# Weight loads of the later experts no longer wait for the rows' transposes, and the planner counts loads, maxima and gathers as ready later

## The chip, the cores and the metric

The kernel runs on one core of a Trainium2 chip. The metric is the device time of one execution in microseconds (us), as the median of several runs. The engines are named as in the profile: PE (TensorE, matmuls), DVE (VectorE), ACT (ScalarE), POOL (GpSimd) and SP (SyncE, which here issues DMAs).

## The reference

A linear attention with a norm, whose output is the input of a mixture of experts; each token goes to one of eight experts with limited places.

```python
kv = np.einsum('bhsd,bhse->bhde', k, v)
out = np.einsum('bhsd,bhde->bhse', q, kv)
rms = np.sqrt(np.mean(out * out, axis=-1, keepdims=True) + 1e-06)
x = out / rms * g_norm                      # N = 4608 tokens of D = 512
...
logits = x @ w_gate
expert_idx = np.argmax(logits, axis=1)      # E = 8
...
h = np.maximum(np.einsum('ecd,edf->ecf', disp, w1), 0.0)   # F = 1024
y = np.einsum('ecf,efd->ecd', h, w2)
...
out[i] = gate_w[i] * y[expert_idx[i], pos[i]]
```

`disp` holds the tokens of each expert, at most capacity of them; the softmax of the logits gives `gate_w`.

## The kernel before

The first third of the span is attention, norm and the routing of tokens. Then the experts follow, ranked by their number of tokens, r = 0 to 7, with a budget of 704 down to 544 rows. Each product is made in two halves of 16 bits: a value is split into a high and a low part, and of the four products three are made (high by high, low by high, high by low).

For expert r, `products(r)` makes the first products `Gemm1`: eight columns of 128 hidden values, each of 24 matmuls over half of the rows (16 with `w1h`, then 8 with `w1l`) into a buffer `hp`. ACT makes `hh` of it (the high part after the maximum with 0), DVE `hl` (the low part). There are two buffers `hp`, so a third column begins only when `hl` of the first is done. Then the second products follow, in tiles of 24 matmuls of 512 columns into one of two banks `yp`; ACT scales a tile into `ysb`, and POOL scatters it to `out` by the places `si`. The last, narrower tile is made turned: `products` of small matmuls, a copy `yt` by DVE and a transpose by PE.

Beside it runs what the next expert needs. `weights(r + 1)` loads `raw1` and `raw2` in four parts each on SP's queue (512 KB a load, L312), takes the maximum of each part on DVE (`am` L328, then `a` L336 and L338 over the parts), turns it across the partitions on PE (`across`, `pt_max` L341), takes the maximum of that on DVE (`bm` L345, `across_max`) and spreads it on PE (`back`, `pt_max` L348); from it DVE makes the scale (`bmax`, `ew`, `p2t`, `sw`, `sg`). With the scale ACT makes the high parts `w1h`, `w2h` (L362) and DVE the low parts `w1l`, `w2l` (L368). There is one buffer for each part of `raw1` and `raw2`.

`rows_beside(r + 1)` gathers the rows of the next expert in blocks of 128: POOL gathers `xg` by a DMA, POOL makes the norm `xm`, ACT casts `pair` (high, L456), POOL makes its low part (L460), and SP transposes `pair` by a DMA into `xs` (L464). `xm` has one buffer, `pair` two, `xg` three. DVE copies the gate `gt` (L437).

What stands in which order on each engine is fixed before the program runs by a planner, `Plan.place`: it is given operations with a cost, dependencies and a key, takes for each engine the one that can begin first (by the key among those that are ready), and counts its end as its start plus its cost, and its readiness for another engine as that end plus a lag. Its outcome is only an order for each engine; on the chip each engine works its own row off, waiting by semaphores. Operations with the key FIRST are taken as soon as they count as ready.

Of the kernel before, what the change touches and what calls it, by code (L numbers as in the profile page):

```python
# [36 lines left out]
LAG = {("T", "T"): 0.0, ("A", "T"): 0.27, ("A", "V"): 0.15, ("V", "P"): 0.16, ("V", "A"): 0.15, ("A", "A"): 0.14,  # L37
       ("V", "V"): 0.13, ("P", "P"): 0.1, ("D", "D"): 0.0, ("D", "T"): 1.1, ("D", "V"): 1.1, ("D", "P"): 1.1, ("D", "A"): 1.1,
       ("P", "D"): 0.3, ("S", "D"): -0.6, ("T", "S"): 0.2}
LAG_ELSE = 0.21  # L40
# [19 lines left out]
WKEYS = ((29.5, 0.3), (38.0, 0.3))  # L60
ON_X = 0


class Hold:

# [14 lines left out]
class Op:  # L80
    def __init__(self, ways, fn, deps, takes, key):
        self.ways, self.fn, self.deps, self.takes, self.key = ways, fn, deps, takes, key
        self.todo, self.next, self.end = 0, [], None


class Plan:
# [14 lines left out]
    def place(self):  # L101
        for n, o in enumerate(self.ops):
            o.n = n
            deps = set(o.deps)
            for h in o.takes:
                if h.before:
                    deps.update(h.before.users)
            o.deps = deps
            for d in deps:
                d.next.append(o)  # L110
            o.todo = sum(d.end is None for d in deps)
        free, order = dict(self.free), []
        ready = {e: [] for e in free}

        def enter(o):
            o.at = {e: max([d.end + LAG.get((d.eng, e), LAG_ELSE) for d in o.deps], default=0.0) for e, _ in o.ways}
            for e, t in o.ways:
                ready[e].append((o, t))

        for o in self.ops:  # L120
            if not o.todo:
                enter(o)
        while len(order) < len(self.ops):
            best = None
            for e, cands in ready.items():
                mine = []
                for o, t in cands:
                    at = max(free[e], o.at[e])
                    if all(at + t <= max(free[f], o.at[f]) + u for f, u in o.ways):
                        mine.append((at, o.at[e] if e in FIFO else o.key, o.n, o, t))  # L130
                if mine:
                    at = min(mine)[0]
                    if best is None or at < best[0]:
                        best = (at, e) + min(x[1:] for x in mine if x[0] <= at + WAIT.get(e, 0.0))
            at, e, _, _, o, t = best
            o.start = max(free[e], o.at[e])
            o.end = free[e] = o.start + t
            o.eng = e
            for f, _ in o.ways:
                ready[f] = [x for x in ready[f] if x[0] is not o]  # L140
            order.append(o)
            for x in o.next:
                x.todo -= 1
                if not x.todo:
                    enter(x)
        self.free = free
        return sorted(order, key=lambda o: (o.start, o.n))
# [8 lines left out]
def attention_moe_kernel(  # L156
# [1318 lines left out]
    def weights(r, key, after):  # L1475

        ws, sets, zs, holds = wsets[r % 2], [], [], []
        for i in range(2):
# [9 lines left out]
            for p in range(4):  # L1488
                o = op(("S", 0.7), lambda e, i=i, p=p, regs=regs: load(e, i, p, regs),
                       [regs.get("op"), early["rank"]] + after + (early["free"][p] if r == 1 and i == 0 else []), key,  # L1490
                       (raws[p],))
                regs.setdefault("op", o)
                loads.append(op(("D", 1.46), None, [o], key, (), (raws[p],)))
            key += 1
            tops = []
            for p in range(8):
# [10 lines left out]
                f["across"](x.t[:, 128:256])  # L1507

            o = op(("V", 0.3), lambda e, f=f: f["most"](), tops, FIRST)
            o = op(("T", 0.12), across, [o], FIRST, (x,))  # L1510
            o = op(("V", 0.2), lambda e, f=f, x=x: f["across_max"](x.t[:, 128:256]), [o], FIRST, (), (x,))
            o = op(("T", 0.03), lambda e, f=f, x=x: f["back"](x.t[:, 0:1]), [o], FIRST, (), (x,))
            ew = new(f"e{i}")
            o = op(("V", 1.1), lambda e, f=f, x=x: f["scale"](x.t[:, 0:1]), [o], FIRST, (ew,), (x,))
# [10 lines left out]
    def rows_beside(r, key):  # L1525
# [9 lines left out]
        for i in range(n):  # L1535
# [7 lines left out]
            o = op(("P", 1.05), fetch, [cut_, first], key, (hold, xg), (sl,))  # L1543
            first = first or o
            o = op(("D", 0.85), None, [o], key, (), (xg,))
            a = op(("P", 1.0), lambda e, i=i: st["x"].norm(i, nc.gpsimd), [o], key + 1, (xm,), (xg,))
            gates.append(op(("V", 0.07), lambda e, i=i: st["x"].gate(i), [o], key + 1, (), (xg, hold)))
            a = op(("A", 0.52), lambda e, i=i: st["x"].pair_high(i), [a], key + 1, (pair,), (xm, hold))
# [58 lines left out]
    for r in range(E):  # L1607
        products(r, *args)
        key = KEY * r
        if r + 1 < E:  # L1610
            sets, zs, w_holds = weights(r + 1, key + 1, sent)
            st, xs_hold, sl, gates, turned, sent = rows_beside(r + 1, key + ROWS)
            args = (lambda st=st: st["x"], turned, turned, gates, xs_hold, lambda st=st: st["si"], sl, sets, zs, w_holds, 0,
                    BUDGET[r + 1])
        else:
            steps, o = plan_rest(), None
            for _ in range(60):
                o = op(("V", 0.2), lambda e: next(steps, None), [o], key + 1)
# [36 lines left out]
```

## Time and profile before

| | |
|---|---|
| median of 3 runs | 613.12 us (611.6 to 616.77) |
| profiled execution | 612.04 us |
| its span in the trace | 610.2 us |
| mean granted clock of TensorE | 0.976 |
| PE busy | 539.9 us (88%) |
| DVE busy | 388.0 us (64%) |
| ACT busy | 258.5 us (42%) |
| POOL busy | 225.1 us (37%) |

Busy times are of the profiled execution, with shares of its span. The median of three runs stands 1.08 us over the profiled one. The shares are averages over stages with different limits, so the single stages are read from the rows below, in which all times count from the span's start.

### The profile page before, as it was taken

Reading aid. Unit: us, or ns where it says so; the run is one execution under the profiler, and the core shown is the slowest. Engines: PE = TensorE matmul, PEld = TensorE weight load, DVE = VectorE, ACT = ScalarE, POOL = GpSimd, SP = SyncE. Lnnn points to the kernel's source line nnn. Section 1 sums busy time; section 2 is a strip of 40 time slices with the busy share of each in tenths; the row PEclk is TensorE's granted clock in tenths of the full one; section 3 lists DMA queues with packets and bytes.
Section 4 is the critical chain, followed back from the end, with each engine's and each line's share of the span. In section 5 each row is a group of like instructions: output and inputs, shape, how many; then the busy total and the mean of one; then the engine's idle time right before and its main releaser. Section 6 shows DMA issues by size and latency. Waiting matters only on the chain.

```text
span 610.2 us, 12003 instructions
## 1 busy us (share of the span) xinstructions
PE 539.9 (88%) x4535; PEld 368.0 (60%) x4535; DVE 388.0 (64%) x1026; ACT 258.5 (42%) x500; POOL 225.1 (37%) x273
## 2 busy tenths in 40 slices
PE   1988989778978987998999899989999999999990
PEld 1887978666535554645764465567477558658650
DVE  2495787999959998889897298059638905102100
ACT  0564767487413922716443515241552534112110
POOL 6002243255336882456308321812652370010010
PEclk9998999999999988999999989999999999999996
DMA  8999999845169687795804750573357141010010
GB/s 217 297 304 334 331 329 367 266 139 212 69 185 333 125 254 173 194 281 128 309 2 117 219 193 15 137 255 119 78 162 277 37 115 22 0 68 5 0 55 8
DMA packets 94654, 102.71 MB, mean 168 GB/s; under 512 B 51650, under 2 KB 76226, under 8 KB 93568
## 3 DMA queue, kind: packets, MB, share of 16 engines
q1 hardware_dynamic: 86528, 70.50, 41.6%
q0 software_dynamic: 8064, 31.40, 14.9%
q8 instruction: 37, 0.61, 0.4%
q14 instruction: 25, 0.20, 0.1%
HBM read 73.20 MB, written 20.68 MB: 154 GB/s over the span
## 4 chain that ended last, share of the span: by engine, by line
DVE 24%; PE 17%; issue 16%; DMA 12%; POOL 7%; ACT 2%; SPq 1%; POOLq 0%; DVEq 0%; ACTq 0%
PE hp L513 9%; DMA out_dram<-ysb,si 6%; DVE am L328 5%; PE yp L559 5%; DVE w2l L368 5%; DVE w1l L368 4%; DVE hl L521 3%; DMA xs<-pair 3%; POOL pair L460 2%; DMA raw<-in_moe_w_dram 2%; DMA xg<-x_dram,gi 2%; POOL out_dram L589 1%; POOL xm L432 1%; PE yp L568 1%; PE op L513 1%
## 5 line engine op out<-in xcount | busy, mean ns | idle before, releaser
L513 PE MATMUL hp<-xs,w1h 128*128 128x320 f16 (+6 forms) x960 | 139.5, 298 | 11.3 <-DVE p2t L293 5.8
L513 PEld LDWEIGHTS <-w1h 128*128 128x128 f16 x1024 | 100.7, 99 | 50.0 <-issue 15.3
L559 PEld LDWEIGHTS <-hh 128*128 128x128 f16 x560 | 54.0, 98 | 64.2 <-issue 1.9
L518 ACT ACTIVATE hh<-hp 128x320 f16<-128x320 f32 (+7 forms) x64 | 40.9, 641 | 117.2 <-PE hp L513 102.7
L589 POOL DMA_INDIRECT out_dram<-ysb,si x42 | 43.8, 1042 | 120.8 <-ACT ysb L584 94.3
L328 DVE TENSOR_REDUCE am<-raw 128x1 f32<-128x512 f32 x120 | 76.0, 674 | 18.5 <-DMA raw<-in_moe_w_dram 18.5
L424 POOL DMA_INDIRECT xg<-x_dram,gi x42 | 44.0, 1047 | 111.1 <-DVE gt L437 70.2
L513 PE MATMUL hp<-xs,w1l 128*128 128x320 f16 (+6 forms) x480 | 72.2, 292 | 0.0
L521 DVE SCALAR_TENSOR_TENSOR hl<-hp,hh 128x320 f16<-128x320 f32 (+7 forms) x64 | 47.4, 741 | 35.8 <-ACT hh L518 35.7
L780 PE MATMUL op<-kv_bd,qt 128*128 128x144 f32 (+1 forms) x384 | 57.8, 293 | 9.2 <-ACT o_sb L663 3.9
L559 PE MATMUL yp<-w2h,hh 128*128 128x512 f16 x272 | 65.2, 379 | 0.8 <-ACT ysb L584 0.8
L559 PE MATMUL yp<-w2h,hl 128*128 128x512 f16 x272 | 64.4, 379 | 0.0
L559 PE MATMUL yp<-w2l,hh 128*128 128x512 f16 x272 | 64.3, 379 | 0.0
L513 PEld LDWEIGHTS <-w1l 128*128 128x128 f16 x512 | 50.3, 98 | 16.9
L368 DVE SCALAR_TENSOR_TENSOR w1l<-raw,sg,w1h 128x512 f16<-128x512 f32 x64 | 58.3, 951 | 0.0
L780 PEld LDWEIGHTS op<-kv_bd,qt 128*128 128x128 f32 x384 | 50.0, 194 | 12.9 <-ACT o_sb L663 5.2
L584 ACT ACTIVATE ysb<-yp,ysc 128x512 f32<-128x512 f32 (+5 forms) x41 | 28.0, 683 | 62.3 <-PE yp L559 48.4
L456 ACT CAST pair<-xm 128x512 f16<-128x512 f32 (+5 forms) x36 | 22.2, 616 | 69.0 <-POOL xm L432 55.1
L460 POOL TENSOR_TENSOR pair<-xm,pair 128x512 f16<-128x512 f32 (+5 forms) x36 | 42.9, 1190 | 20.4 <-ACT pair L456 19.8
L574 DVE COPY yt<-yp 128x256 f32<-128x256 f32 (+4 forms) x7 | 2.9, 415 | 73.6 <-PE yp L568 61.3
L432 POOL TENSOR_TENSOR xm<-xg 128x512 f32<-128x512 f32 (+5 forms) x39 | 45.0, 1156 | 11.8 <-DMA xg<-x_dram,gi 10.0
L559 PEld LDWEIGHTS <-hl 128*128 128x128 f16 x280 | 27.2, 98 | 32.7 <-issue 0.9
(242 smaller groups left out, 730.6 us busy)
## 6 DMA issues: line engine op xcount, KB each, us to landing
raw<-in_moe_w_dram SPq DMA_DIRECT2D x64, 512.0 KB
x_dram<-o_sb POOLq DMA_DIRECT2D x8, 1152.0 KB, 4.7
k_sb<-in_k_dram SPq DMA_DIRECT2D x16, 512.0 KB
v_sb<-in_v_dram SPq DMA_DIRECT2D x16, 512.0 KB
q_sb<-in_q_dram SPq DMA_DIRECT2D x16, 512.0 KB
x_dram<-o_sb POOLq DMA_DIRECT2D x8, 144.0 KB, 8.5
k_sb<-in_k_dram SPq DMA_DIRECT2D x16, 64.0 KB
v_sb<-in_v_dram SPq DMA_DIRECT2D x16, 64.0 KB
```

What stands on the lines that cost most here:

```text
L328: nc.vector.tensor_reduce(out=am()[:, p:p + 1], in_=raw[:, sl(p)], axis=AX.X, op=ALU.max, apply_absolute_value=True)
L368: nc.vector.scalar_tensor_tensor(out=wl[:, sl(p)], in0=raw[:, sl(p)], scalar=z["s"], in1=wh[:, sl(p)], op0=ALU.mult, op1=ALU.subtract)
L424: nc.gpsimd.indirect_dma_start(out=self.xg[i][0:n], out_offset=None, in_=x_dram[0:self.rows, :], in_offset=bass.IndirectOffsetOnAxis(ap=se ...
L432: eng.tensor_tensor(out=self.xm[i][0:n].rearrange("p (h d) -> p h d", h=H), in0=xg[:, :, 0:D], in1=xg[:, :, D:D + 1].broadcast_to([n, H, D ...
L460: nc.gpsimd.tensor_tensor(out=pair[0:n, 1], in0=self.xm[i][0:n], in1=pair[0:n, 0], op=ALU.subtract)
L513: nc.tensor.matmul(self.view(hp)[:, u], lhsT=w[:, c, j * P:(j + 1) * P], rhs=x[:, c, u * hw:(u + 1) * hw], start=(t == 0 and c == 0), stop ...
L518: nc.scalar.activation(self.out(self.hh, j), self.view(hp), AF.Relu)
L521: nc.vector.scalar_tensor_tensor(out=self.out(self.hl, j), in0=self.view(hp), scalar=0.0, in1=self.out(self.hh, j), op0=ALU.max, op1=ALU.s ...
L559: nc.tensor.matmul(yp[0:n, 0:DM], lhsT=h[:, j, o:o + n], rhs=w[:, j, :], start=(m == 0), stop=(m == len(self.terms) - 1))
L584: nc.scalar.activation(self.ysb[0:n], yp[0:n, 0:DM], AF.Copy, scale=self.ysc[0:n, i:i + 1])
L589: nc.gpsimd.indirect_dma_start(out=out[:, :], out_offset=bass.IndirectOffsetOnAxis(ap=self.sidx[0:n, col:col + 1], axis=0), in_=ysb[0:n], ...
L780: nc.tensor.matmul(ph.t[:, j * m:(j + 1) * m], lhsT=qt.t[:, i * P:(i + 1) * P], rhs=x, start=True, stop=True)
```

## The change

A constant `LATE` is added, and each operation gets a value `late`, 0 if nothing else is said. The planner adds it to the end of an operation when it works out when the ones that depend on it are ready. It is 4.0 us for the landing of a weight load, 2.0 us for `most` (which makes `a`) and 1.0 us for `across_max` (which makes `bm`), all for the weights of the experts 2 to 7, and 1.1 us for the landing of a gather of rows. And `weights` of the experts 3 to 7 no longer gets `sent`, the transposes of the rows of expert r, as something that its loads wait for.

```diff
+LATE = (4.0, 2.0, 1.0)
...
-        self.todo, self.next, self.end = 0, [], None
+        self.todo, self.next, self.end, self.late = 0, [], None, 0.0
...
-            o.at = {e: max([d.end + LAG.get((d.eng, e), LAG_ELSE) for d in o.deps], default=0.0) for e, _ in o.ways}
+            o.at = {e: max([d.end + d.late + LAG.get((d.eng, e), LAG_ELSE) for d in o.deps], default=0.0) for e, _ in o.ways}
...
                 loads.append(op(("D", 1.46), None, [o], key, (), (raws[p],)))
+                loads[-1].late = LATE[0] if r > 1 else 0.0
...
             o = op(("V", 0.3), lambda e, f=f: f["most"](), tops, FIRST)
+            o.late = LATE[1] if r > 1 else 0.0
             o = op(("T", 0.12), across, [o], FIRST, (x,))
             o = op(("V", 0.2), lambda e, f=f, x=x: f["across_max"](x.t[:, 128:256]), [o], FIRST, (), (x,))
+            o.late = LATE[2] if r > 1 else 0.0
...
             o = op(("D", 0.85), None, [o], key, (), (xg,))
+            o.late = 1.1
...
-            sets, zs, w_holds = weights(r + 1, key + 1, sent)
+            sets, zs, w_holds = weights(r + 1, key + 1, [] if r > 1 else sent)
```

No operation is added or taken away. The lines of the changed kernel stand two to six further down (L312 becomes L314, L521 becomes L523). The orders differ from `products(0)` on, at about 189 us of the span.

The first place is on SP, beside the second products of expert 2: `xs` are the rows of expert 4, `raw1` the first weights of expert 5, `raw2` the last load of expert 4's weights. Before:

```order
L312 DMA raw2_2643<-in_moe_w2_dram 128x2x512
L464 DMA_TRANSPOSE xs_4428<-pair_4485 128x8x128
L1420 TENSOR_LOAD n_i_4517
L1420 ISA x2
L464 DMA_TRANSPOSE xs_4428<-pair_4531 128x8x128
L464 DMA_TRANSPOSE xs_4428<-pair_4579 128x8x128
L464 DMA_TRANSPOSE xs_4428<-pair_4607 128x8x128
L464 DMA_TRANSPOSE xs_4428<-pair_4629 128x8x80
L1485 TENSOR_LOAD perm_i_145
L1485 ISA x2
L312 ISA
L312 DMA raw1_149<-in_moe_w1_dram 128x1024
```

In the changed kernel the same stretch of SP:

```order
L314 DMA raw2_2643<-in_moe_w2_dram 128x2x512
L1487 TENSOR_LOAD perm_i_145
L1487 ISA x2
L314 ISA
L314 DMA raw1_149<-in_moe_w1_dram 128x1024
...
L314 DMA raw1_149<-in_moe_w1_dram 128x1024
L466 DMA_TRANSPOSE xs_4422<-pair_4495 128x8x128
L314 ISA
L314 DMA raw1_149<-in_moe_w1_dram 128x1024
L1422 TENSOR_LOAD n_i_4434
```

Three of the four loads of `raw1` now stand ahead of the first transpose, the fourth behind it; the other four transposes follow.

The second place is on DVE at the start of the products of expert 3, where `am0`, `a1_0` and `bm` belong to the weights of expert 5, `w2l` to those of expert 4, and `hl` to the first column. Before:

```order
L437 COPY gt_4429<-xg_4529 80x1
L328 TENSOR_REDUCE am0_4676<-raw1_149 128x1 x2
L368 SCALAR_TENSOR_TENSOR w2l_0_153<-raw2_2643,sw1_4439,w2h_0_152 128x512 x5
L521 SCALAR_TENSOR_TENSOR hl_4738<-hp_4678,hh_4737 128x624
L293 TENSOR_SCALAR p2t_4763<-ew0_3831 128x1
```

In the changed kernel the same place on DVE:

```order
L439 COPY gt_4423<-xg_4549 80x1
L330 TENSOR_REDUCE am0_4553<-raw1_149 128x1 x2
L338 TENSOR_REDUCE a1_0_4640<-am0_4553 128x1
L340 TENSOR_TENSOR a1_0_4640<-a1_0_4640,gcol_124 128x1
L347 TENSOR_REDUCE bm_4670<-pt_max_4664 1x1
L370 SCALAR_TENSOR_TENSOR w2l_0_153<-raw2_2643,sw1_4504,w2h_0_152 128x512 x5
L523 SCALAR_TENSOR_TENSOR hl_4752<-hp_4693,hh_4751 128x624
```

The other six `am0` of the eight stand further ahead of this piece; before, they came between the `hl` of this expert's later columns.

The third place is on DVE in the first products of expert 1, where `am0`, `a1_0`, `am1` and `bm` belong to the weights of expert 2; the first `hl` of the piece before is that of the third column (`hp_3406`). Before:

```order
L328 TENSOR_REDUCE am0_3319<-raw1_149 128x1 x3
L1344 TENSOR_REDUCE nt_3453<-big_3367 128x9
L336 TENSOR_REDUCE a1_0_3455<-am0_3319 128x1
L338 TENSOR_TENSOR a1_0_3455<-a1_0_3455,gcol_124 128x1
L521 SCALAR_TENSOR_TENSOR hl_3351<-hp_3406,hh_3350 128x672
L328 TENSOR_REDUCE am1_3337<-raw2_2643 128x1 x2
L345 TENSOR_REDUCE bm_3482<-pt_max_3471 1x1
```

In the changed kernel, where `hp_3409` is the third column and `hp_3444` the fourth:

```order
L523 SCALAR_TENSOR_TENSOR hl_3363<-hp_3409,hh_3362 128x672
L330 TENSOR_REDUCE am0_3407<-raw1_149 128x1 x3
L1351 TENSOR_TENSOR upto_3344<-upto_3344,nt_3345 128x1
L338 TENSOR_REDUCE a1_0_3491<-am0_3407 128x1
L340 TENSOR_TENSOR a1_0_3491<-a1_0_3491,gcol_124 128x1
L523 SCALAR_TENSOR_TENSOR hl_3363<-hp_3444,hh_3362 128x672
L330 TENSOR_REDUCE am1_3420<-raw2_2643 128x1 x2
L1351 TENSOR_TENSOR upto_3344<-upto_3344,nt_3345 128x1
L439 COPY gt_3050<-xg_3367 128x1
L1351 TENSOR_TENSOR upto_3344<-upto_3344,nt_3345 128x1 x2
L347 TENSOR_REDUCE bm_3532<-pt_max_3518 1x1
```

`a1_0` and `bm` each stand one column later on DVE. On PE `across` moves from within the fourth column to behind the fifth, `back` from between the fourth and the fifth into the sixth; and the transposes of `yt` of expert 0, which stood behind the first column of expert 1, now stand ahead of it.

## Rows read from the trace of the kernel before

**Rows 1.** Windows: span, length, each engine's busy time, PEclk (granted clock), DMA share, GB/s.

```profile
216.60:255.00 38.40, 32.75 (x209) 21.02 (x206) 32.71 (x77) 18.05 (x29) 21.24 (x18) 0.91 0.78 194
...
287.70:341.77 54.07, 53.85 (x329) 31.43 (x325) 41.81 (x93) 21.46 (x34) 21.82 (x20) 1.00 0.46 145
341.77:399.16 57.39, 53.77 (x392) 34.14 (x391) 31.50 (x70) 22.10 (x35) 21.81 (x20) 0.97 0.49 142
```

**Rows 2.** Timeline of PE, first products of expert 1: start, us, operation, [idle before, releaser].

```profile
218.94 3.98 PE L513 MATMUL hp<-xs,w1h 128*128 128x336 f16 x15 [2.03 <-DMA xs<-pair]
...
238.79 0.38 PE L348 MATMUL pt_max<-bm,ones 1*128 1x1 f32 x2 [3.04 <-DVE bm L345]
239.10 4.09 PE L513 MATMUL hp<-xs,w1h 128*128 128x336 f16 x16
...
244.21 2.44 PE L513 MATMUL hp<-xs,w1h 128*128 128x336 f16 x16
```

**Rows 3.** Windows behind three of PE's idle times.

```profile
238.79:242.98 4.19, 4.18 (x18) 2.46 (x19) 4.02 (x13) 2.47 (x4) 1.21 (x2) 0.61 0.44 97
...
351.90:355.60 3.70, 3.68 (x16) 2.15 (x16) 3.56 (x11) 0.00 (x0) 0.00 (x0) 0.56 0.69 226
218.94:222.75 3.81, 3.81 (x16) 2.12 (x17) 3.74 (x13) 0.00 (x0) 2.56 (x3) 0.55 0.77 237
```

**Rows 4.** Timeline of PE, second products of expert 1.

```profile
269.92 0.38 PE L348 MATMUL pt_max<-bm,ones 1*128 1x1 f32 x2 [0.83 <-DVE bm L345]
...
271.96 1.89 PE L559 MATMUL yp<-w2h,hh 128*128 128x512 f16 x8
...
276.15 0.27 PE L341 MATMUL pt_max<-ident,a 128*1 128x128 f32 x1 [0.57 <-DVE a L336]
...
278.40 0.38 PE L348 MATMUL pt_max<-bm,ones 1*128 1x1 f32 x2 [1.11 <-DVE bm L345]
```

**Rows 5.** Timeline of PE, first products of the experts 3, 4 and 5.

```profile
344.95 2.28 PE L513 MATMUL hp<-xs,w1h 128*128 128x312 f16 x16
...
351.92 3.91 PE L513 MATMUL hp<-xs,w1h 128*128 128x312 f16 x16 [3.62 <-DVE p2t L293]
...
407.49 2.17 PE L513 MATMUL hp<-xs,w1h 128*128 128x296 f16 x16 [1.69 <-DVE p2t L293]
...
411.28 2.17 PE L513 MATMUL hp<-xs,w1h 128*128 128x296 f16 x16 [0.61 <-DVE hl L521]
...
465.11 2.12 PE L513 MATMUL hp<-xs,w1h 128*128 128x288 f16 x16 [0.97 <-DVE hl L521]
```

**Rows 6.** Timeline of DVE, first products of the experts 3, 4 and 5.

```profile
346.56 1.28 DVE L328 TENSOR_REDUCE am<-raw 128x1 f32<-128x512 f32 x2 [14.38 <-DMA raw<-in_moe_w_dram]
347.75 3.39 DVE L368 SCALAR_TENSOR_TENSOR w2l<-raw,sw,w2h 128x512 f16<-128x512 f32 x5
...
403.41 0.69 DVE L328 TENSOR_REDUCE am<-raw 128x1 f32<-128x512 f32 x1 [3.38 <-DMA raw<-in_moe_w_dram]
...
463.04 0.35 DVE L623 COPY si<-sidx_tab 128x6 int32 x1 [2.20 <-DMA out_dram<-ysb,si]
```

**Rows 7.** Timeline of SP's DMA issues: start, time from the first issue to the last.

```profile
324.06 16.84 SPq L464 DMA_TRANSPOSE xs<-pair  x5
342.07 14.11 SPq L312 DMA_DIRECT2D raw<-in_moe_w_dram  x8
```

**Rows 8.** Timeline of ACT, first products of the experts 1 and 3.

```profile
235.24 0.62 ACT L456 CAST pair<-xm 128x512 f16<-128x512 f32 x1 [6.56 <-DMA xs<-pair]
...
342.56 3.17 ACT L362 ACTIVATE w2h<-raw,sw 128x512 f16<-128x512 f32 x5
```

**Rows 9.** The chain that ended last: start, us, what.

```profile
222.82 12.32 DMA xs<-pair
...
236.51 0.86 DVE hl L521
...
494.30 3.12 DMA xs<-pair
```

## Prediction

> **What bounds the kernel now.** I read the windows first, by expert. From 216.60 us on, when the experts ranked 1 to 7 follow each other, TensorE (PE) works almost without a break: 53.85 of 54.07 us beside expert 2, 53.77 of 57.39 beside expert 3, but only 32.75 of 38.40 in the first products of expert 1 [rows 1]. In the fullest of these windows VectorE (DVE) has 41.81 of 54.07, so PE sets the pace, and the only time to win after 216 us is where PE stands still or runs at the lower of its two clocks. I therefore went through PE's timeline for the idle times in brackets, and from each to the engine named as its releaser.
>
> Three places stand out. In the products of expert 1, PE waits 2.03 us for the first rows, then 3.04 us for the maximum `bm` [rows 2]. In the second products of expert 1 it waits 0.83, 0.57 and 1.11 us for `bm` and `a` [rows 4]. Then each of the experts 3, 4 and 5 has a wait in its first columns: 3.62, 1.69 and 0.61, 0.97 us [rows 5]. After two of these idle times the clock falls as well: the 16 matmuls that take 2.44 us at 244.21 took 4.09 behind the wait of 3.04, with a granted clock of 0.61; those that take 2.28 at 344.95 took 3.91 behind the wait of 3.62, with 0.56 (of the level of 2.4 GHz, so near that of 1.2) [rows 2, 3, 5]. Behind the wait of 1.69 us 16 matmuls of 296 columns took 2.17, as usual [rows 5].
>
> Where the long waits come from is read on DVE. At 346.56 its queue had been standing for 14.38 us at a maximum `am` whose weight load had not landed; behind it came five `w2l` (3.39 us), and only then `hl`, which frees the first buffer `hp`, which PE wants for its third column [rows 6]. SP shows why the load was late: its eight loads were issued from 342.07 on, behind the five transposes that began at 324.06 [rows 7]. At 403.41 the same `am` wait is 3.38 us [rows 6].
>
> **Experts 3 and 4: the waits for a load.** With the dependency gone three of the four `raw1` loads stand ahead of the first transpose on SP, and with the new late times the planner puts all eight `am`, `a1` and `bm` ahead of the `w2l`. The data is loaded some 15 to 20 us sooner (in the place of transposes from 324.06 on, instead of 342.07 [rows 7]), so the `am` has its data while the second products of the expert before still run, and DVE was idle for those 14.38 us. What is late next: `w2l` needs `w2h` from ScalarE (ACT), whose five run from 342.56 for 3.17 us [rows 8], so the fifth `w2l` ends near 345.7 + 0.7 = 346.4 (3.39 us for five is 0.7 each) and `hl` 0.8 later at 347.2. PE's second column ends at 351.92 - 3.62 = 348.3, so 1.1 us are left, and the whole wait goes. Expert 3: 3.62 + (3.91 - 2.28) for the clock = 5.25, 5.3 with the eight `w1l` behind it that ran a little slow too. Expert 4: 1.69 + 0.61 = 2.3. Nothing in these two sums is on another engine's path.
>
> **Expert 5.** Here DVE stood 2.20 us for a scatter to `out` that still read the old `si`, then did two `am`, and `hl` came late by 0.97 us [rows 6, 5]. The wait for the scatter is not touched; the two `am` (1.27 us) move ahead to the second products before. I take the whole 0.97 as 1.0. Bounds: 0, if the scatter alone makes `hl` late, and 1.0.
>
> **Second products of expert 1.** The waits add to 0.83 + 0.57 + 1.11 = 2.51 us [rows 4]. The late times move `across` and `back` some 12 to 16 matmuls (2.6 to 3.5 us) further back on PE, which covers each of them, if DVE does not come later too. DVE is the tight engine here, its `am` waiting for loads that still follow rows' transposes (expert 3's are issued earlier, but their buffer is freed by `w1l` of expert 2). I take 1.5, bounds 0 and 2.5.
>
> **First products of expert 1.** PE's wait of 3.04 us is for `bm`, which sits on DVE behind `hl` of the third column (236.51 to 237.37) and two `am` [rows 2, 9]. In the new order `across` comes after the fifth column and `back` within the sixth, so the fifth column no longer stands behind `bm` but only behind the third `hl`, at 237.4 instead of 239.10: 1.7 us. That `hl` stays where it was: ACT stood 6.56 us at a cast for a transpose that was issued at 222.82 behind five loads and took 12.32 us, with the `hh` of this column queued behind the cast [rows 8, 9]; nothing in this part of SP's order changes. The fourth column ended at 239.10 - 0.31 - 3.04 = 235.75, so PE now waits 1.6 us there, and since 1.69 us left the clock alone [rows 5] and 2.03 us did not (0.55 after it [rows 3]), I count the slow 16 matmuls as saved: 4.09 - 2.44 = 1.65. Together 3.4. Bounds: 0, if the wait stays over 2 us and the clock falls, or the maxima now wait inside the next columns; 5, if the whole wait with its clock goes. One step here is against the change: the transposes of `yt` of expert 0 now stand ahead of the first column, and `yt` is copied on DVE behind `w2l`, so PE may start its first column later than 218.94. Up to 1.6 us of that cost nothing, since they only shorten the wait for the third `hl` at 237.4; what is more comes off the 3.4, one for one, within its bounds.
>
> **Expert 2.** Its window has 0.22 us of idle PE to give [rows 1], and receives eight `am` of 0.64 us (half of the 1.28 for two [rows 6]) from the window behind: DVE goes from 41.81 to about 46.9 of 54.07. I count a loss of 0.4, bounds 0 and 1.5 (two `hl` late by one `am` each). The 1.1 us by which gathers count as late move only where their readers stand in the queues; POOL and its DMAs keep their order, and I price it at 0.
>
> **The sum.** 5.3 + 2.3 + 1.0 + 1.5 + 3.4 - 0.4 = 13.1 us. The profiled execution took 612.04 us (span 610.2 and 1.84 around it), 1.08 under the median of 613.12. So 612.04 - 13.1 = 598.9, and 613.12 - 13.1 = 600.0 as a median. With every bound at its best it is 5.3 + 2.3 + 1.0 + 2.5 + 5 = 16.1, so 597.0; with the open ones at their worst 5.3 + 2.3 + 0 + 0 + 0 - 1.5 = 6.1, so 607.
>
> **Rivals.** *The transposes are late instead.* Three sets of transposes (rows of experts 4, 5, 6) now queue behind three or four loads of 512 KB. One behind five loads took 12.32 us, one alone 3.12 [rows 9]. `pair` has two buffers, so the third cast on ACT waits for the first transpose; transposes are 16.84 / 4 = 4.2 us apart [rows 7], so the cast is due 8.4 us after the first one's issue and would wait 3.9. Behind it ACT holds an output `ysb`, and PE with its two buffers `yp` can run one tile of 24 matmuls further, under 3 x 1.89 = 5.7 us [rows 4]. So 3.9 us alone are hidden. It decides if SP, at a load whose buffer the last `w1l` have not yet freed, stands for more than 6 us besides: more than a whole set of eight such DVE operations (0.7 each). At 8 us PE would wait 3.9 + 8 - 5.7 = 6.2, with a slow clock (1.65) 7.9 for each of three experts: 23.6 - 13.1 gives 10.5 slower, 623.6. Against it: the window of expert 3 has DMA engines busy for 0.49 only [rows 1], and the `w1l` are done well before the transposes begin. The Trainium skill has a rule on this side: by "DMA: Bandwidth & Descriptors", section "Queues, rings and completion order", what SP issues lies on one ring on each of the DMA engines and is taken in ring order, so a transpose cannot pass the loads ahead of it. The 12.32 us row agrees with it; by it each of the three sets would be delayed as that row was, which is the 3.9 us above.
>
> *Only the experts 3 to 5 gain.* In expert 1 the order of maxima and `hl` is so dense that what leaves one place waits in the next: the third `hl` and the gather of expert 2's rows are unmoved. Then 5.3 + 2.3 + 1.0 = 8.6 and 604.5.
>
> *The change doesn't do what it says.* The `am` comes early, but `hl` is late all the same, since the `w2l` ahead of it are paced by `w2h`: from the margin of 1.1 us above, it takes only a `w2h` group that begins 1.2 us later than 342.56 for the wait to return. Then experts 3 and 4 keep theirs, and with 1.5 or less from the rest the time is 611 to 613.
>
> **How the numbers follow.** The forecast of 600.0 gets 0.63, the gain in experts 3 to 5 alone (604.5) 0.20, no effect (612) 0.12, late transposes (623.6) 0.05. 1% of this kernel is 6.1 us, about what a measurement of it can tell from no change; so faster by over 1% means under 607.0: nearly all of the first case and most of the second, with some of the spread off, 0.77; within 1% what is left of these and the third, 0.18; slower 0.05. The range leaves the last two cases out, and reaches from 595.5 (the best sum, 597.0, less the 1.5 by which the fastest run of before lies under the median) to 608.5 (the worst sum, 607.0, and the same).
>
> **What would show it.** In the trace of the changed kernel: no wait of PE in the third column of experts 3 and 4, and a clock of 1.00 there; `am` on DVE without a long wait for `raw` between 332 and 347; the loads of experts 5, 6 and 7 ahead of the transposes on SP, and these longer, with ACT's casts waiting for `xs<-pair` by up to 4 us without PE following. In expert 1 a wait of about 1.6 us or less ahead of the fifth column, released by `hl`, without a fall of the clock. The windows of experts 6 and 7 should last as long as before. I am wrong if PE shows new idle times with `ysb` as releaser (late transposes), if the waits in expert 1 only move on to the sixth column or the next tile, or if `hl` in expert 3 still ends after 348.3.

## The result and the profile after

The changed kernel took 605.61 us in the median of four runs (603.92 to 608.32), the kernel before 612.42 beside it: a ratio of 0.9895 with a 95% interval of 0.9853 to 0.9936, so about 6.4 us less. Ratios leave disturbed executions out and can differ from the quotient of the medians. The profiled execution took 605.59 us with a span of 603.8. The time lies in the range of the prediction (595.5 to 608.5), its direction is right, and the 13.1 us of the sum are twice what came.

The windows of the changed kernel by expert, cut where the first matmul of each stage begins (the first two rows are the first and the second products of expert 1, then the experts 2 to 5; the first row begins where the products of expert 0 end), with the columns of [rows 1]:

```profile
218.95:256.45 37.50, 30.22 (x201) 20.29 (x201) 31.70 (x75) 13.47 (x22) 20.81 (x19) 0.95 0.83 211
256.45:290.84 34.39, 30.05 (x226) 15.07 (x224) 31.69 (x65) 15.79 (x27) 17.64 (x15) 0.97 0.72 195
290.84:345.39 54.55, 54.55 (x333) 32.02 (x330) 46.75 (x107) 22.16 (x36) 22.49 (x22) 0.99 0.63 183
345.39:397.30 51.91, 51.91 (x391) 33.57 (x390) 31.62 (x71) 20.11 (x33) 20.20 (x19) 1.00 0.54 150
397.30:447.11 49.81, 49.81 (x396) 32.78 (x395) 31.00 (x72) 20.82 (x34) 20.94 (x20) 1.00 0.59 160
447.11:496.21 49.10, 48.33 (x393) 31.69 (x392) 25.12 (x60) 22.20 (x37) 23.73 (x22) 1.00 0.46 122
```

Beside the experts 2, 3 and 4 PE is now busy in the whole window. Expert 3 went from 57.39 us [rows 1] to 51.91. The two windows of expert 1 did not get shorter together: 71.9 us where before had 71.1. The timeline of PE in expert 1 shows why:

```profile
223.90 1.03 PE L581 MATMUL yp<-ident,yt 128*64 128x128 f32 x4 [4.95 <-DVE t_e L1315]
...
242.11 2.44 PE L515 MATMUL hp<-xs,w1h 128*128 128x336 f16 x16 [2.34 <-DVE hl L523]
...
279.53 0.38 PE L350 MATMUL pt_max<-bm,ones 1*128 1x1 f32 x2 [1.68 <-DVE bm L347]
...
287.97 0.38 PE L350 MATMUL pt_max<-bm,ones 1*128 1x1 f32 x2 [2.67 <-DVE bm L347]
...
290.84 2.90 PE L515 MATMUL hp<-xs,w1h 128*128 128x320 f16 x16
```

These rows answer to [rows 2] and [rows 4]. The wait of 3.04 us for `bm` in the first products is gone, with its slow clock, but 4.95 us stand ahead of the first column (for the copy `yt`; the name of the releaser is that of the instruction beside it on DVE) and 2.34 ahead of the fifth. The second products wait 1.68 + 2.67 where before waited 2.51 in three pieces, and the last wait is followed by a slow first column of expert 2 (2.90 us for 16 matmuls, 2.33 in the kernel before). DVE in the same stretch, and in expert 3:

```profile
214.93 8.29 DVE L370 SCALAR_TENSOR_TENSOR w2l<-raw,sw,w2h 128x512 f16<-128x512 f32 x8
...
223.34 0.41 DVE L576 COPY yt<-yp 128x256 f32<-128x256 f32 x1
...
241.19 0.86 DVE L523 SCALAR_TENSOR_TENSOR hl<-hp,hh 128x672 f16<-128x672 f32 x1 [3.94 <-ACT hh L520]
...
278.06 0.15 DVE L439 COPY gt<-xg 128x1 f32<-128x1 f32 x1 [2.25 <-DMA xg<-x_dram,gi]
...
281.80 0.15 DVE L338 TENSOR_REDUCE a<-am 128x1 f32<-128x8 f32 x1
...
287.65 0.27 DVE L347 TENSOR_REDUCE bm<-pt_max 1x1 f32<-1x128 f32 x1
...
346.92 3.40 DVE L370 SCALAR_TENSOR_TENSOR w2l<-raw,sw,w2h 128x512 f16<-128x512 f32 x5 [5.78 <-ACT w2h L364]
350.24 0.80 DVE L523 SCALAR_TENSOR_TENSOR hl<-hp,hh 128x624 f16<-128x624 f32 x1
```

Between `a` and `bm` at 281.80 and 287.65 DVE works without a wait, mostly on small steps for the tables of places and on a `w1l`; PE's second wait for `bm` is for these. The last two rows answer to [rows 6]: in expert 3 DVE no longer waits for a load, but for `w2h` of ACT, and `hl` ends at 351.04. The timeline of PE there, with the third column last, is without a bracket:

```profile
348.57 2.28 PE L515 MATMUL hp<-xs,w1h 128*128 128x312 f16 x16
350.69 1.22 PE L515 MATMUL hp<-xs,w1l 128*128 128x312 f16 x8
351.75 2.28 PE L515 MATMUL hp<-xs,w1h 128*128 128x312 f16 x16
```

So `hl` comes 0.7 us before the third column, where the prediction had estimated 1.1. The casts of ACT, in expert 1 (first row, which answers to [rows 8]) and beside the second products of expert 2:

```profile
239.91 0.62 ACT L458 CAST pair<-xm 128x512 f16<-128x512 f32 x1 [6.22 <-DMA xs<-pair]
...
329.47 0.62 ACT L458 CAST pair<-xm 128x512 f16<-128x512 f32 x1 [3.52 <-POOL xm L434]
...
336.36 0.62 ACT L458 CAST pair<-xm 128x512 f16<-128x512 f32 x1 [5.69 <-POOL xm L434]
```

In expert 1 the wait for the transpose behind five loads is still 6.22 us; beside the experts 2 to 4 the casts wait for POOL and not for a transpose.

### The profile page after: what moved, and what is told of

It is laid out like the page before. It is cut to its first block, busy times and chain, and to the rows that moved or that the text cites. A ratio compares the mean times of both kernels' runs of the same rounds, so it can differ in the third digit from the quotient of the medians.

```text
span 603.8 us, 11995 instructions
## 1 busy us (share of the span) xinstructions
PE 540.7 (90%) x4535; PEld 373.0 (62%) x4535; DVE 386.5 (64%) x1026; ACT 257.6 (43%) x500; POOL 222.9 (37%) x273
## 4 chain that ended last, share of the span: by engine, by line
PE 34%; DVE 23%; DMA 15%; issue 14%; POOL 5%; ACT 3%; SPq 3%; POOLq 0%; DVEq 0%; ACTq 0%
PE hp L515 15%; PE yp L561 8%; DMA out_dram<-ysb,si 6%; PE op L782 4%; DVE w1l L370 4%; DMA q_sb<-in_q_dram 4%; DVE am L330 4%; DVE w2l L370 3%; PE qp L764 2%; DMA xs<-pair 2%; DVE hl L523 2%; DMA xg<-x_dram,gi 2%; SPq L679 1%; DVE ss L811 1%; POOL pair L462 1%
## 5 line engine op out<-in xcount | busy, mean ns | idle before, releaser
L515 PE MATMUL hp<-xs,w1h 128*128 128x320 f16 (+6 forms) x960 | 135.9, 294 | 5.3 <-DVE hl L523 2.7
L523 DVE SCALAR_TENSOR_TENSOR hl<-hp,hh 128x320 f16<-128x320 f32 (+7 forms) x64 | 47.4, 741 | 42.0 <-ACT hh L520 42.0
L782 PE MATMUL op<-kv_bd,qt 128*128 128x144 f32 (+1 forms) x384 | 60.1, 301 | 5.7 <-ACT qt L665 2.3
L458 ACT CAST pair<-xm 128x512 f16<-128x512 f32 (+5 forms) x36 | 22.1, 615 | 86.8 <-POOL xm L434 77.5
L782 PEld LDWEIGHTS op<-kv_bd,qt 128*128 128x128 f32 x384 | 52.4, 203 | 9.1 <-ACT o_sb L665 3.5
L370 DVE SCALAR_TENSOR_TENSOR w2l<-raw,sw,w2h 128x512 f16<-128x512 f32 x64 | 47.6, 794 | 9.5 <-ACT w2h L364 9.5
L370 DVE SCALAR_TENSOR_TENSOR w1l<-raw,sg,w1h 128x512 f16<-128x512 f32 x64 | 52.5, 862 | 0.0
L561 PEld LDWEIGHTS <-hl 128*128 128x128 f16 x280 | 27.3, 98 | 33.2 <-issue 0.9
```

The costliest lines, as they stand in the source:

```text
L370: nc.vector.scalar_tensor_tensor(out=wl[:, sl(p)], in0=raw[:, sl(p)], scalar=z["s"], in1=wh[:, sl(p)], op0=ALU.mult, op1=ALU.subtract)
L515: nc.tensor.matmul(self.view(hp)[:, u], lhsT=w[:, c, j * P:(j + 1) * P], rhs=x[:, c, u * hw:(u + 1) * hw], start=(t == 0 and c == 0), stop ...
L523: nc.vector.scalar_tensor_tensor(out=self.out(self.hl, j), in0=self.view(hp), scalar=0.0, in1=self.out(self.hh, j), op0=ALU.max, op1=ALU.s ...
L561: nc.tensor.matmul(yp[0:n, 0:DM], lhsT=h[:, j, o:o + n], rhs=w[:, j, :], start=(m == 0), stop=(m == len(self.terms) - 1))
L782: nc.tensor.matmul(ph.t[:, j * m:(j + 1) * m], lhsT=qt.t[:, i * P:(i + 1) * P], rhs=x, start=True, stop=True)
```

## The experiments

The account to be tried is that the experts 3 to 5 gain since the loads go ahead of the transposes, and that expert 1 loses what was expected of it, through `yt`, the third `hl` and `bm`. Each run tries a part of it, with a theory 1 and a theory 2 of its own. The lengths of the stages below are differences of the starts of their first matmuls in PE's timelines, in us (first products of expert 1 from the end of expert 0's, second products of expert 1, then experts 2 to 5):

| kernel | exp. 1 first | exp. 1 second | 2 | 3 | 4 | 5 | ratio to before, 95% |
|---|---|---|---|---|---|---|---|
| before | 38.4 | 32.7 | 54.07 | 57.39 | 52.62 | 50.10 | 1 |
| before again (e8) | 41.0 | 32.7 | 53.76 | 55.63 | 52.46 | 49.86 | |
| changed | 37.5 | 34.4 | 54.55 | 51.91 | 49.81 | 49.10 | 0.9895 (0.9853 to 0.9936) |
| changed again (e5) | 42.4 | 30.7 | 54.21 | 51.92 | 49.80 | 49.56 | 0.9872 (0.9799 to 0.9944) |
| dependency alone (e1) | 38.1 | 30.7 | 57.51 | 53.02 | 50.33 | 48.00 | 0.9995 (0.9947 to 1.0043) |
| the same again (e7) | 37.6 | 31.9 | 63.17 | 52.80 | 51.91 | 48.00 | |
| late times alone (e2) | 41.4 | 31.0 | 53.68 | 51.93 | 50.74 | 52.63 | 0.9936 (0.9891 to 0.998) |
| late from expert 4 (e3) | 37.9 | 30.8 | 53.98 | 51.92 | 49.87 | 49.61 | 0.9899 (0.9868 to 0.9931) |
| gathers late from 2 (e4) | 37.8 | 31.0 | 55.08 | 51.91 | 50.90 | 49.59 | 0.9884 (0.9855 to 0.9914) |
| e4 and third `pair` (e6) | 34.1 | 35.4 | 54.07 | 51.91 | 49.80 | 48.82 | 0.9825 (0.9755 to 0.9896) |
| e6, gathers 5.0 late (e9) | 35.2 | 30.3 | 56.49 | 53.36 | 51.09 | 49.66 | 0.9856 (0.9796 to 0.9917) |
| before, third `pair` (e10) | 37.6 | 33.2 | 53.97 | 57.07 | 51.68 | 50.05 | 0.9947 (0.9901 to 0.9993) |
| only loads late (e11) | 40.2 | 32.3 | 58.77 | 52.65 | 52.25 | 48.08 | 1.0015 (0.997 to 1.0059) |
| changed, third `pair` (e12) | 35.6 | 30.9 | 54.24 | 51.91 | 50.69 | 49.60 | 0.9805 (0.9748 to 0.9862) |

The stages of a row are those of one execution, while the medians below and the ratios are of all runs of a kernel; the execution of e1 was the fastest of nine. The intervals of most of the ratios overlap.

**e1, the dependency alone.**

```diff
-LATE = (4.0, 2.0, 1.0)
+LATE = (0.0, 0.0, 0.0)
...
-            o.late = 1.1
+            o.late = 0.0
```

> The dependency of the loads on the transposes is gone, all late times are 0. Theory 1 (the waits of PE in the experts 3 to 5 end because the loads are issued before the transposes): the `am` wait of 14.4 us on DVE in front of the third column of expert 3 is gone, PE's wait of 3.62 us there too, and the time is near 605 (8 us less than 612.4); the first products of expert 1 stay as before, with PE waiting about 3 us for `bm`. Theory 2 (the late times do it, since they put `hl` and `w2l` where their inputs are): without them `am` and `bm` stand ahead of their data again, PE gets new waits for `bm` in the experts 2 to 5, and the time is 609 to 613.

612.54 us (604.97 to 619.25) beside 613.82: no gain, as theory 2 says of the time. PE's waits in the first columns of the experts 3 and 4 are gone, as theory 1 says, but the second products of expert 2 are 2.8 us longer in this execution, and 8.5 us in that of e7, through new waits as theory 2 says (for `a`, more than for `bm`). **e7** is the same kernel once more.

> e1 once more, for its profile: its profiled execution (604.97) was 7.6 us under its own median. Theory 1: the attention's part makes the scatter, so this profile is longer mostly ahead of 217 us. Theory 2: without late times `am` and `bm` stand just where their loads land, so the experts' stages differ from run to run, by waits of PE for `a` and `bm` that one profile has and the other has not.

It took 611.65 us, 6.7 us more than the execution of e1, of which expert 2 makes 5.7, and the part ahead of 217 us was the same within 0.9 (216.94 against 217.8): theory 2. The timelines of PE and DVE in e7 show the new wait:

```profile
335.10 0.27 PE L343 MATMUL pt_max<-ident,a 128*1 128x128 f32 x1 [4.23 <-DVE a L340]
```

```profile
333.38 1.28 DVE L330 TENSOR_REDUCE am<-raw 128x1 f32<-128x512 f32 x2 [1.83 <-DMA raw<-in_moe_w_dram]
```

The maxima moved ahead with the loads, PE's `across` with them, and PE now waits for `a` in the second products: the wait is only moved.

**e2, the late times alone.**

```diff
-            sets, zs, w_holds = weights(r + 1, key + 1, [] if r > 1 else sent)
+            sets, zs, w_holds = weights(r + 1, key + 1, sent)
```

> The late times stay, the loads wait for the transposes as in the kernel before. Theory 1: the loads of expert 5 are issued after the transposes, at about 340, and DVE or PE still waits for them near the third column of expert 3; 609 to 613. Theory 2: DVE has no `am` ahead of its `w2l` there, so PE's waits of 3.62 and 1.69 us go although the loads are as late as before; 605 or less. For expert 1 both expect what the changed kernel shows: PE waits some 4 to 5 us for the transposes of `yt`, and 4 us for `bm` in the second products.

608.83 us (603.61 to 613.06), ratio 0.9936: between the two theories; in expert 3 theory 2 is right. The loads are as late as before, yet expert 3 takes 51.93 us, since `am` of expert 5's weights now stands behind the first `hl` and not ahead of the `w2l`. What is missing against the changed kernel in this execution is in the experts 4 and 5 (50.74 and 52.63 us): there DVE's queue stands at the old `si` (2.46 and 3.87 us), with two `am` behind it and only then `hl`, and PE's timeline has:

```profile
409.10 2.17 PE L515 MATMUL hp<-xs,w1h 128*128 128x296 f16 x16 [0.75 <-DVE hl L523]
...
461.05 3.51 PE L515 MATMUL hp<-xs,w1h 128*128 128x288 f16 x16 [2.27 <-DVE hl L523]
```

In expert 1 the wait for `yt` is there as expected (4.96 us), but that for `bm` in the second products is 1.15 us and not 4.

**e11, only the loads late.**

```diff
-LATE = (4.0, 2.0, 1.0)
+LATE = (4.0, 0.0, 0.0)
```

> The changed kernel with LATE = (4, 0, 0): the landings of loads are counted late, `a` and `bm` are not. Theory 1 (what e1 lacked are the maxima, which stood on DVE and PE ahead of loads that had not landed): with 4 us for the loads alone PE's waits of 2 to 4 us for `a` in the second products of the experts 2 to 4 are gone or under 0.5 us, and the time is that of the changed kernel, 604 to 607. Theory 2 (the rows' other work on DVE holds `a` and `bm`, and the 2.0 and 1.0 us cover that): waits of 1 us and more for `a` and `bm` in the experts 2 to 4 stay, 608 to 611.

616.82 us (610.0 to 623.83), ratio 1.0015; theory 2, and in the median worse than its 608 to 611. PE waits 3.06 and 2.29 us for `a` in the second products of the experts 2 and 4. DVE shows that no load was late; other work stood among the maxima, and the last step of `a` took 0.87 us in place of 0.16:

```profile
335.64 1.27 DVE L330 TENSOR_REDUCE am<-raw 128x1 f32<-128x512 f32 x2
336.82 0.78 DVE L1414 TENSOR_TENSOR zrow<-zrow,tok 128x40 f32<-128x40 f32 x1
337.64 1.08 DVE L1417 CAST zrow_i<-zrow 128x40 int32<-128x40 f32 x1
338.65 0.14 DVE L439 COPY gt<-xg 80x1 f32<-80x1 f32 x1
338.71 1.26 DVE L330 TENSOR_REDUCE am<-raw 128x1 f32<-128x512 f32 x2
340.00 0.16 DVE L338 TENSOR_REDUCE a<-am 128x1 f32<-128x8 f32 x1
340.20 0.87 DVE L340 TENSOR_TENSOR a<-a,gcol 128x1 f32<-128x1 f32 x1
```

So without the dependency the 2.0 and 1.0 us on `a` and `bm` are needed, as the changed kernel differs from e11 by them alone: with them PE does not stand at `a` in these places.

**e3, late times from expert 4 on.**

```diff
-                loads[-1].late = LATE[0] if r > 1 else 0.0
+                loads[-1].late = LATE[0] if r > 3 else 0.0
...
-            o.late = 1.1
+            o.late = 1.1 if r > 3 else 0.0
```

(and the same condition for `LATE[1]` and `LATE[2]`.)

> The late times hold from the weights and rows of expert 4 on; the loads from expert 3 on do not wait for transposes. On PE the products of expert 1 stand as in the kernel before. Theory 1 (what the changed kernel lacks of the forecast was lost in expert 1: Gemm2 1.7 us longer than before, Gemm1 hardly shorter, and some 2 us ahead of it that belong to the scatter of the attention's part and not to the change): expert 1 takes 71 us as before, experts 3 to 5 gain 8 to 9, and the time is 603 to 604. Theory 2 (the late times in expert 1 are worth something that the scatter hides): 606 or more, as much as the changed kernel or slower.

603.74 us (602.07 to 608.32), ratio 0.9899: as theory 1 in the time, but expert 1 takes 68.7 us and not the 71 that theory 1 gave it. In the ratio it can't be told from the changed kernel: the late times beside expert 1 bring nothing, and cost nothing beyond the scatter.

**e5 and e8, the two kernels again.**

> The changed kernel once more, word for word, beside the others of this call. Theory 1 (the 2.2 us by which everything stood later at 183 us of the span are scatter of the attention's part; the losses in expert 1 are the change's own): in this profile too PE waits some 4 to 5 us for `yt`, over 2 us for the third `hl` and over 2 us for `bm` of expert 3's weights, and expert 1 takes about 72 us from the end of expert 0's products; the time is 0.988 to 0.991 of before. Theory 2 (these waits are scatter too): they differ by over 2 us in sum from the first profile.

> The kernel before once more, for a second profile. Theory 1: PE's waits of 3.6 and 1.7 us in the experts 3 and 4 stand there again, since they come from the order on SP; only the time ahead of 217 us differs, by up to 4 us. Theory 2: they are smaller or gone in this execution, and the gain in experts 3 to 5 is partly scatter.

e8 (611.86 us): the waits in the experts 3 and 4 are there again (3.54, 1.54 and 0.62 us), so their gain is the change's; only the slow clock of expert 3 is not there again. e5: 605.65 us (603.56 to 605.98). The 4.95 us for `yt` are there again to the hundredth, the third `hl` is late by 3.54 in place of 2.34, and for `bm` PE waits only 0.89 in place of 1.68 + 2.67. So the wait for `yt` belongs to the change, and the other two differ by 1.2 and 3.5 us between two executions of one kernel. One matmul on PE near 183 us, where the orders do not differ yet, stands at 185.38 in the first profile of the changed kernel and at 184.19 here, at 183.05 and 184.48 in those of before: these 2.3 us between the first profiles are scatter too.

**e4, gathers of expert 1 not late.**

```diff
-            o.late = 1.1
+            o.late = 1.1 if r > 1 else 0.0
```

> As the changed kernel, but the gathers of expert 1's rows are not counted 1.1 us late; with that the transposes of `yt` stand behind the first column again. Theory 1 (the wait for `yt` of 4.95 us delayed all of expert 1's first products): PE waits 2 us for the first rows as before instead, the first products of expert 1 end about 1 to 2 us sooner, and the time is 604. Theory 2 (the third `hl`, behind ACT's cast that waits for a transpose, sets the end of these products whatever stands ahead): no difference to the changed kernel, 605 to 606.

603.47 us (601.77 to 604.22), which is nearer to theory 1, while the ratio of 0.9884 beside 0.9895 and 0.9872 shows no difference, as theory 2 says. `yt` stands behind the first column again, and the first products take 37.8 us, as in the first profile of the changed kernel (37.5). The wait for the third `hl` is 2.35 us, as there, but 16 slow matmuls follow it (3.97 us in place of 2.44), and that `hl` ends 21.5 us after the products of expert 0 in place of 23.1 and 25.4. One reason stands on DVE ahead of it, in a row that took 8.29 us in the changed kernel:

```profile
215.32 7.08 DVE L370 SCALAR_TENSOR_TENSOR w2l<-raw,sw,w2h 128x512 f16<-128x512 f32 x8
```

These eight `w2l` take 8.29 us in the five profiles in which the gathers of expert 1 are counted late (the changed kernel, e2, e5, e11, e12), and 7.08 in the nine others.

**e6, e10 and e12, a third buffer `pair`** (with e4, the kernel before and the changed kernel; the orders of all engines stay).

```diff
-            self.pair[i] = self.pool.tile([P, 2, DM], F16, name="pair", bufs=2)
+            self.pair[i] = self.pool.tile([P, 2, DM], F16, name="pair", bufs=3)
```

> As e4, but with three buffers `pair` instead of two; all orders are the same. Theory 1 (the third `hl` of expert 1 is late since ACT stands 6 us at a cast that waits for a transpose behind five loads, with `hh` behind it): that cast no longer waits, PE's wait of 2.35 us for `hl` at 240 and the slow clock after it (3.97 instead of 2.44) go, 3.5 to 4 us less than e4: 599.5 to 600, or 0.982 to 0.983 of before. Theory 2 (DVE with its `w2l` and the loads' landing set the end of these products): ACT's wait goes, but PE then waits for `bm` or `a` instead, and the time is within 1.5 us of e4.

> The kernel before with three buffers `pair`, nothing else. Theory 1: in expert 1 ACT's wait of 6.6 us at the cast goes, and `hl` of the third column comes in time, but `bm` stands on DVE right behind and PE waits for it less than 3 us; experts 3 to 5 keep their waits; 609 to 611. Theory 2 (the third buffer is worth the 4 us by itself, or even more, and has nothing to do with the change): 606 to 608.

> The changed kernel with three buffers `pair`, all orders the same. Theory 1 (the third `hl` hid what the transposes of `yt` ahead of the first column cost): without the late `hl` the 4.95 us for `yt` count, and the time lies 1.5 to 3 us above e6 and 1 to 2.5 below the changed kernel: 603 to 604.5. Theory 2 (the third `hl` was all): 601 to 602, as e6.

e6: 601.87 us (599.6 to 602.74), 1.6 less than e4, where theory 1 said 3.5 to 4. It is 3.8 less than the changed kernel (e5), whose runs all lie above it, but from that it differs by the gathers of expert 1 as well. ACT no longer waits for a transpose, and PE's timeline has 0.20 us for the fifth column, and the first products take 34.1 us in place of 37.8, as theory 1 says; but the second products then wait 2.83 us for `bm`, as theory 2 says, with a slow clock behind it (35.4 us in place of 31.0):

```profile
235.47 2.44 PE L515 MATMUL hp<-xs,w1h 128*128 128x336 f16 x16 [0.20 <-DVE hl L523]
...
273.16 0.58 PE L350 MATMUL pt_max<-bm,ones 1*128 1x1 f32 x2 [2.83 <-DVE bm L347]
...
275.35 3.62 PE L561 MATMUL yp<-w2h,hh 128*128 128x512 f16 x8
```

DVE in e6 shows what `bm` stood behind, a copy `gt` of a gather that had not landed:

```profile
272.69 0.15 DVE L439 COPY gt<-xg 128x1 f32<-128x1 f32 x1 [5.08 <-DMA xg<-x_dram,gi]
272.76 0.15 DVE L1351 TENSOR_TENSOR upto<-upto,nt 128x1 f32<-128x1 f32 x1
272.83 0.27 DVE L347 TENSOR_REDUCE bm<-pt_max 1x1 f32<-1x128 f32 x1
```

e10: 610.84 us, ratio 0.9947; as theory 1, the third buffer alone is worth some 2 to 3 us, since `bm` follows (1.26 us). e12: 602.79 us (602.23 to 603.24), ratio 0.9805. All its runs lie below all runs of the changed kernel (603.56 us and more), from which it differs by the third buffer alone. Its time lies between the ranges of the two theories, 0.9 over e6; by the stages the first products of expert 1 take 35.6 us against 34.1, so that the wait for `yt`, with the longer `w2l`, costs 1.5 us there, as theory 1 says, which the shorter second products (30.9 against 35.4) more than make up in these two executions.

**e9, gathers 5.0 us late.**

```diff
-            o.late = 1.1 if r > 1 else 0.0
+            o.late = 5.0 if r > 1 else 0.0
```

> As e6 (three `pair`, gathers of expert 1 not late), but the gathers from expert 2 on are counted 5.0 us late instead of 1.1, so that on DVE `bm` of expert 3's weights stands ahead of the fourth copy `gt` instead of behind it. Theory 1 (in the second products of expert 1 PE waits for `bm` because DVE's queue stands at `gt`, whose gather takes 9 to 12 us where the planner counts 2): PE's wait of 2.83 us there and the slow matmuls after it are gone, the second products take about 31 us instead of 35.4, and the time is 597 to 599. Theory 2 (the maxima themselves are late, since the loads land late): a wait of 2 us or more for `bm` or `a` stays, 601 to 602.

606.36 us (604.45 to 607.18), ratio 0.9856. At its place theory 1 is right: with `bm` ahead of `gt` the wait is 0.85 us, and the second products take 30.3 us. But the time did not follow: the experts 2, 3 and 4 are 1.3 to 2.4 us longer than in e6, with new waits in their third columns, here that of expert 3 and the next:

```profile
349.70 2.28 PE L515 MATMUL hp<-xs,w1h 128*128 128x312 f16 x16 [0.95 <-DVE p2t L295]
353.22 2.28 PE L515 MATMUL hp<-xs,w1h 128*128 128x312 f16 x16 [0.18 <-DVE hl L523]
```

Of the 7.5 us by which this execution is longer than that of e6, 4.2 stand ahead of expert 1 (220.28 against 216.06). The number that mended one place shifted others.

## Why the prediction was right in sign and twice what came

**Experts 3 and 4: right in place, and in size where the clock was slow.** Predicted 5.3 and 2.3 us; from the first profiles 5.48 and 2.81 came, from the second ones (e8 and e5) 3.71 and 2.66. In expert 3 the difference between the two is mostly the slow clock, which one execution of before had and the other had not. What was late next was named rightly (`w2h`). The step "with the dependency gone" gives only half of the reason: e2 shows that the late times alone bring expert 3's gain with the loads as late as before, and e1 that the removed dependency alone brings it too, but gives it back in the second products of expert 2 (57.51 and 63.17 us). In the ratio neither part alone reaches the 6 to 8 us of both (e1 0.3 us, e2 3.9, whose interval overlaps with that of both).

**Expert 5:** predicted 1.0, measured 1.0 and 0.3; the 1.0 is luck. The wait for `si`, held to be untouched, is gone (DVE has no bracket at `si`), but the first `hl` now comes late, since DVE waits 2.44 and 2.89 us for `w2h` of ACT. PE waits 0.41 + 0.36 us in these columns, and 0.87 + 0.36 in the second profile, where before had 0.97 and 0.73 in one piece. The rest of the 1.0 is that PE is busy for 48.33 us in this window in place of 48.94; one of the two sets of maxima has moved to the window before.

**Second products of expert 1:** predicted a gain of 1.5 us; measured a loss of 1.7 and a gain of 2.0. The step "some 12 to 16 matmuls further back on PE, which covers each of them, if DVE does not come later too" fell on its condition: DVE came later. At the first of the two waits for `bm` (1.68 us) it had stood at `gt` for a gather, 2.25 us in the first profile and 5.08 in e6, and e9 shows that this is the cause at that place. At the second (2.67 us; 0.89 in the other profile) it had no wait, but the small steps and a `w1l` from 281.80 to 287.65. That `bm` begins at 287.65 and 287.87 in the two profiles, though the first products ended 3.75 us apart (256.45 and 260.20): in these two DVE sets this end, and what PE gains ahead of it comes back as a wait. So the two halves of expert 1 are better read together: a gain of 4.9 was predicted, a loss of 0.8 and a gain of 0.6 came. That the waits in expert 1 move on to the next tile was one of the prediction's own signs of being wrong.

**First products of expert 1:** predicted a gain of 3.4; measured 0.9 and a loss of 1.4. The step that failed is "That `hl` stays where it was". Counted from the end of expert 0's products it ended at 20.8 and 22.1 us in the two executions of before, and at 23.1 and 25.4 in those of the changed kernel: the eight `w2l` took 8.29 us in place of 7.08 (in both pairs of profiles), with the transpose behind them issued later (7.3 us after expert 0's products in both, before 6.2 and 6.9), and it took longer (13.56 and 15.88 us by the chain, before 12.32 and 12.96). The chain of the changed kernel:

```profile
226.25 13.56 DMA xs<-pair
239.91 0.62 ACT pair L458
240.53 0.64 ACT hh L520
241.19 0.86 DVE hl L523
```

e6 beside e4, and e12 beside the changed kernel, show that this transpose, through ACT's cast, makes the third `hl` late: with a third `pair` PE waits for it 0.20 us in e6 and not at all in e12. The move of `yt`, held to cost nothing up to 1.6 us, hid behind it; without the late `hl` it costs 1.5 us in e12. The longer `w2l` come from the gathers of expert 1, which were counted late, as e4 shows: the prediction had priced these late gathers at 0, since "POOL and its DMAs keep their order", and POOL's timeline has a scatter to `out` one `xm` further ahead there than before. By what way this lengthens the `w2l` is not shown: the median of the eight is 0.74 us in both kernels, the longest takes 1.96 in the changed kernel and 1.64 in before, and that of the changed kernel, from 221.3 us on, runs beside an `xm` of POOL (221.58 to 222.66). Nor is it shown why the transpose takes longer.

**Expert 2:** predicted a loss of 0.4, measured 0.48 and 0.45; DVE has 46.75 of 54.55 us, predicted 46.9. No `hl` came late, as the prediction had priced it: PE has no wait there in the first profile, and the slow first column (0.57 us) is as much as the whole loss; in the second PE is busy for 54.14 us in place of 53.69, at the full clock.

**The rivals.** The transposes behind the loads cost nothing in the experts 2 to 4, where no cast of ACT waits for one; they land after 3.8 us in the median and 9.4 at most. The ring order of "DMA: Bandwidth & Descriptors" (the Trainium skill, "Queues, rings and completion order") agrees with the trace in expert 1, where the cast waited 6.22 us behind five loads, but the delay that the prediction drew from it for each set did not come. The result, 605.61, lies nearest to the second rival (only the experts 3 to 5 gain, 604.5), which had 0.20. The sum by the first profiles: 5.48 + 2.81 + 1.00 - 0.48 - 1.69 + 0.90 is 8.0; 0.7 more in the experts 6 and 7, which e8 has as well, so they are not the change's; and 2.35 lost ahead of expert 1, of which 2.33 stood there at 183 us already, before the orders differ, so they are scatter: 6.4. That the time lies in the range rests on its lower end, which had put the open terms at nothing: the experts 3 to 5 carry the gain, and the 4.9 us of expert 1 did not come.

## What to carry to other kernels

When a wait at the head of an in-order queue is removed, ask of each reader behind it what it waits for next, and count that from the measured duration of its own input, not from where it stood before. A planner's late times and its dependencies work together: an earlier load moves its maxima, and their PE steps, ahead of data that the plan only believes to be there. A buffer more in a ring that couples a DMA queue to a busy engine (here `pair`) takes the coupling away without touching the order; with it the changed kernel came to 602 to 603 us, while the next wait, for `bm`, took a part of the gain back in e6.

## What the runs showed of the hardware

Whether the clock falls behind a wait of PE could not be told from the wait's length here. Behind 2.27 us (e2, expert 5) and 2.35 (e4) 16 matmuls took 3.51 and 3.97 in place of 2.12 and 2.44; behind 2.34 (the changed kernel) and 3.40 (e11) they took 2.44, as at the full clock. The same 3.54 us went both ways, in e8 and in e5, each with the window behind it:

```profile
354.59 2.28 PE L513 MATMUL hp<-xs,w1h 128*128 128x312 f16 x16 [3.54 <-DVE p2t L293]
```

```profile
354.59:356.90 2.31, 2.31 (x18) 1.72 (x18) 2.17 (x9) 0.00 (x0) 0.00 (x0) 1.00 0.80 284
```

```profile
243.22 4.64 PE L515 MATMUL hp<-xs,w1h 128*128 128x336 f16 x16 [3.54 <-DVE hl L523]
```

```profile
243.22:247.90 4.68, 4.68 (x17) 2.52 (x17) 4.61 (x13) 0.62 (x1) 2.12 (x3) 0.50 0.74 142
```

So the step of the prediction that took a wait of over 2 us for one that costs the clock does not hold as a rule: in the first profile the clock did not fall behind 2.34 us, in e5 the 16 matmuls behind 3.54 us took 2.2 us more. Against its taking 1.6 us for safe nothing here speaks: waits of 1.54 (e8), 1.67 (e6) and 1.69 us ahead of a column were followed by the full clock. Small operations of DVE (128 by 40 values and less) took about 0.2 us in one place and 0.8 to 1.9 in another, as `a` in the rows of e11; a cause is not shown.
